# Batch 0's start in a fused attention and GEGLU kernel: small zero products, constants made in another order, masks put off, first gate block halved

## The chip, the cores and the metric

The kernel runs on one core of one Trainium2 chip. The metric is the device time of one execution, in microseconds, as the median of several executions. The core's engines run in parallel, each through its own queue in order: TensorE (PE, with its weight loads as PEld), VectorE (DVE), ScalarE (ACT), GpSimd (POOL), and SyncE (SP). POOL, ACT and SP also issue DMAs.

## What is computed

The reference is an attention block with a sliding window, followed by a gated feed-forward block, in float32:

```
scores = q @ k^T / sqrt(64) - slope[h] * |i - j|
attn   = softmax(scores where 0 <= i - j < 128)      # 8 batches, 8 heads, 576 positions, 64 wide
x      = (attn @ v), heads side by side               # 4608 tokens x 512
out    = (gelu(x @ w_gate) * (x @ w_val)) @ w_out     # 512 -> 1536 -> 512
```

## The kernel before, in words

All engines run in the order in which the program is written (`manual_schedule`, L52); nothing is reordered by a scheduler. Waits come from the data: an instruction waits for the producers of what it reads, and for the last readers of what it overwrites. PSUM has eight banks, taken in rotation by `bank()` (L70): taking a bank means waiting until the reads of its last content, eight takes before, are done.

The work has two interleaved streams. Attention goes batch by batch. Scores are held transposed (keys on partitions), 256 queries per 128 keys; `exp` on ACT (L211) writes them to `P` in bfloat16; a multiplication with `emask` on DVE (L214, `mask`) applies the slope and the window. The denominators are products of `P` with selecting constants (`ones4`, `ones8`, `sums4`, L342), then a reciprocal on DVE, then products with `sel` or `sel8` that spread the reciprocals over partitions (`spread4`, L383). `values` (L440) multiplies `P` with v and normalises into `xT`, the transposed tokens of the second stream. That stream goes by groups of 512 tokens: `gate_val(g, f, lo, hi)` (L467) makes one 128-row block f of the hidden layer, for the tokens lo to hi, from four products with w_gate and four with w_val, gelu on ACT (L481) and a product on DVE (L482); there are 12 blocks in a group. `out_part` (L495) makes the outputs. From batch 1 on, the mixing is written in `todo` and `steps`, which the change leaves alone.

Batch 0, where the change lies, is written out by hand at L526 to L645, to start the core as early as possible:

- Two lines load q and k in several pieces (`load_runs`), then v (`load_v`), then the weights (`load_w`), all from POOL. Each uses one of eight completion slots in turn, so a DMA is issued only when the DMA eight places before has landed.
- PE first runs products of zeros while nothing has landed: `keep_busy(8)` at L607 makes the next `bank()` issue 8 products of 128x512.
- DVE makes constants: memsets, `ident`, `dist`, `slopes` (L543 to L561). ACT makes `emask[:, h, 0:256]` (L553).
- `first` (L596) transposes q and k for positions 0 to 383 on PE and copies them from PSUM on DVE (`untangle`, L164). Batch 0's first scores get their bias as a product (`biases0`, L256) and need no mask.
- `made_later` (L570) on DVE: two memsets of padding, the copies of `emask` to columns 256 to 511, `sel0`, `sel`.
- `rest` (L601) does the same as `first` for positions 384 to 575; `made_last_part` (L580): `sel8`, `ones8`.
- `scores0_rest` (L275): the scores of the second part, with their exponentials and, at once, their masks. `sums4(0, 0)`, `products_first` and `spread_first` (L453, L458) give xT for tokens 0 to 383. Then come gate blocks f = 0, 1, 2 for these 384 tokens, with the second part's `sums4(0, 1)`, `spread4(0, 1)` and `values(0, 1)` between them, then blocks 0, 1, 2 for tokens 384 to 511 (L644), and from f = 3 whole blocks of 512.

Of the kernel before, what the change touches and what calls it, by code (L numbers as in the profile page):

```python
# [8 lines left out]
BF16 = mybir.dt.bfloat16  # L9
AF = mybir.ActivationFunctionType  # L10
ALU = mybir.AluOpType
# [21 lines left out]
def kernel(  # L33
# [10 lines left out]
    nc = tc.nc  # L44
# [25 lines left out]
    def bank():  # L70
        ps = psum.tile([128, 512], FP32, name="ps")
        for _ in range(heat.pop()):
            nc.tensor.matmul(out=ps.rearrange("p (n x) -> p n x", n=4), lhsT=zeros,
                             rhs=zeros.unsqueeze(1).to_broadcast((128, 4, 128)),
                             start=True, stop=True)
        heat.append(0)
        return ps

    def keep_busy(n):
        heat[0] = n  # L80
# [5 lines left out]
    ident = consts.tile([128, 128], BF16, name="ident")  # L86
# [8 lines left out]
    ones8 = consts.tile([128, 4 * 40], BF16, name="ones8")  # L95


    emask = consts.tile([128, H, 512], BF16, name="emask")
    sel0 = consts.tile([128, 8], FP32, name="sel0")
    sel = consts.tile([128, 8, 64], FP32, name="sel")  # L100
    sel8 = consts.tile([128, 4, 64], FP32, name="sel8")
# [4 lines left out]
    qT, kT = ([consts.tile([128, 4, 640], BF16, name=f"{nm}T{i}") for i in range(2)]  # L106
              for nm in "qk")
    vb = [consts.tile([128, 5, DM], BF16, name=f"vb{i}") for i in range(2)]
# [22 lines left out]
    def runs(what, b, n):  # L131
        first, parts, r = RUNS[b][n]
        t, lo, p = (qs, ks)[what][b], 1536 * n, 0
        if (b, n) == (0, 1):
            t, lo, p = vb[1], 0, 64 * what
        return t.rearrange("p j x -> p (j x)")[p:p + parts, lo:lo + 512 * r].rearrange(
            "p (h x) -> p h x", h=H)
# [15 lines left out]
    def transpose_runs(b, n, what, c, ps):  # L153
        first, parts, r = RUNS[b][n]
        src = runs(what, b, n)
        p = 64 * what if (b, n) == (0, 1) else 0
        for x in range(r):
            for i in (0, 1):
                nc.tensor.transpose(
                    out=ps[64 * i:64 * i + 64, parts * x:parts * x + parts],  # L160
                    in_=src[:, 2 * c + i, 64 * x:64 * x + 64],
                    identity=ident[p:p + parts, p:p + parts])

    def untangle(copy, b, n, what, c0, c1, ps):  # L164
        first, parts, r = RUNS[b][n]
        m = c1 - c0
        copy(out=(qT, kT)[what][b][:, c0:c1, first:first + parts * r].rearrange(  # L167
                 "p c (x r) -> p c x r", r=r),
             in_=ps[:, 0:m * parts * r].rearrange("p (c r x) -> p c x r", c=m, r=r))
# [43 lines left out]
    def mask(dst, m):  # L213
        nc.vector.tensor_tensor(out=dst, in0=dst, in1=m, op=ALU.mult)  # L214
# [41 lines left out]
    def biases0(cs):  # L256
        pss = []
        for c in cs:
            ps = [bank(), bank()]
            pss.append(ps)  # L260
            for i in (0, 1):
                bias(2 * c + i, ps[i], 2)
        return pss
# [8 lines left out]
                exp(prob(0)[:, c, i, 0:512], ps[i])  # L272


    def scores0_rest(cs):  # L275
        pss = []
        for c in cs:
            ps = [bank(), bank()]
            pss.append(ps)
            for j, q0, n, col in ((2, 384, 128, 0), (3, 384, 192, 128), (4, 512, 64, 320)):  # L280
                for i in (0, 1):
                    score(0, c, i, j, q0, n, ps[i][:, col:col + n])
        P = prob(0)
        for c, ps in zip(cs, pss):
            for i in (0, 1):
                exp(P[:, c, i, 640:1024], ps[i][:, 0:384])
            mask(P[:, c, :, 640:1024], emask[:, 2 * c:2 * c + 2, 128:512])


    def biases0_2():  # L290
# [6 lines left out]
    def scores0_2(pss):  # L297
        for c in range(4):
            for i in (0, 1):
                added(c, i, 2, 256, 128, pss[i][:, 128 * c:128 * c + 128])  # L300
        for i in (0, 1):
            exp(prob(0)[:, :, i, 512:640], pss[i].rearrange("p (c n) -> p c n", c=4))
# [164 lines left out]
    def gate_val(g, f, lo=0, hi=512, later=None):  # L467
        if g not in hid:
            hid[g] = h_pool.tile([128, NF, 512], BF16, name="hT")
        t0 = 512 * g % RING  # L470
        n = hi - lo
        pg, pv = bank()[:, 0:n], bank()[:, 0:n]
        for w, ps in ((wg, pg), (wv, pv)):
            for c in range(4):
                nc.tensor.matmul(  # L475
                    out=ps, lhsT=w[:, c, 128 * f:128 * (f + 1)],
                    rhs=xT[:, c, t0 + lo:t0 + hi], start=(c == 0), stop=(c == 3))

        def act():
            gl = g_pool.tile([128, 512], BF16, name="gelu")  # L480
            nc.scalar.activation(out=gl[:, 0:n], in_=pg, func=AF.Gelu)  # L481
            nc.vector.tensor_tensor(out=hid[g][:, f, lo:hi], in0=pv, in1=gl[:, 0:n],  # L482
                                    op=ALU.mult)

        if later is None:
            act()
        else:
            later.append(act)
# [37 lines left out]
    zeros = consts.tile([128, 128], BF16, name="zeros")  # L526
# [16 lines left out]
        nc.vector.memset(slope1[:, h:h + 1], -8.0 * 2.0 ** (-8.0 * (h + 1) / H))  # L543
    nc.vector.memset(ones4, 0.0)
    nc.vector.memset(ones4.rearrange("p (h x) -> p h x", x=36)[:, :, 0:4], 1.0)
    nc.vector.tensor_single_scalar(out=ident, in_=tmpl[:, 0:128], scalar=0.0, op=ALU.is_equal)
    for lo, bound, op in ((0, 0.0, ALU.is_lt), (128, 127.5, ALU.is_gt)):
        nc.vector.tensor_scalar(out=far[:, lo:lo + 128], in0=tmpl[:, lo:lo + 128],
# [7 lines left out]
    def made_slopes(lo, hi):  # L556
        nc.vector.tensor_tensor(
            out=slopes[:, lo:hi, :], in0=ident.unsqueeze(1).to_broadcast((128, hi - lo, 128)),
            in1=slope1[:, lo:hi].unsqueeze(2).to_broadcast((128, hi - lo, 128)), op=ALU.mult)
# [7 lines left out]
        load_runs(1, n, 0, 8)  # L567
    load_w(1280, DFF)

    def made_later():  # L570
        nc.vector.memset(kT[0][:, :, 576:640], 0.0)
        nc.vector.memset(vb[0][64:128, 4, :], 0.0)
        for to, lo, n in ((256, 0, 192), (448, 0, 64)):
            nc.vector.tensor_copy(out=emask[:, :, to:to + n], in_=emask[:, :, lo:lo + n])
        nc.vector.tensor_reduce(
            out=sel0, in_=ident.rearrange("p (g h r) -> p h g r", g=4, r=4)[:, :, :, 0],
            op=ALU.add, axis=mybir.AxisListType.X)
        nc.vector.tensor_copy(out=sel, in_=sel0.unsqueeze(2).to_broadcast((128, 8, 64)))

    def made_last_part():  # L580
        nc.vector.tensor_copy(
            out=sel8, in_=sel0[:, 0:8:2].unsqueeze(2).to_broadcast((128, 4, 64)))
        nc.vector.memset(ones8, 0.0)
        nc.vector.memset(ones8.rearrange("p (h x) -> p h x", x=40)[:, :, 0:8], 1.0)

    def made_last():
        nc.vector.memset(ones, 0.0)
        for i, lo, hi in ((0, 0, 4), (1, 4, 8), (0, 8, 16), (1, 16, 32)):
            nc.vector.memset(ones[:, i, lo:hi], 1.0)
        nc.vector.memset(kT[1][:, :, 576:640], 0.0)  # L590
        nc.vector.memset(vb[1][64:128, 4, :], 0.0)


    act, dve = nc.scalar.copy, nc.vector.tensor_copy

    def first(w, c, copy, ps):  # L596
        ps = ps.bitcast(BF16)
        transpose_runs(0, 0, w, c, ps)
        untangle(copy, 0, 0, w, c, c + 1, ps)
# [4 lines left out]
            transpose_runs(0, 1, w, c, ps[:, 192 * n:192 * n + 192])  # L604
        untangle(copy, 0, 1, w, cs[0], cs[-1] + 1, ps)

    keep_busy(8)  # L607
    held = [bank() for _ in range(4)]
    for c in (0, 1):
        first(0, c, dve, held[c])  # L610
    ps0 = biases0((0,))
    for c in (0, 1):
        first(1, c, dve, held[2 + c])
    made_slopes(4, 8)
    ps0 += biases0((1,))
    scores0((0, 1), ps0)
    held = [bank() for _ in range(4)]
    for w in (0, 1):
        for c in (0, 1):
            first(w, 2 + c, dve, held[2 * w + c])  # L620
    ps0 = biases0((2, 3))
    made_later()
    scores0((2, 3), ps0)
    ps0 = biases0_2()
    scores0_2(ps0)
    for cs in ((0, 1), (2, 3)):
        for w in (0, 1):
            rest(w, cs, dve)
    made_last_part()
    row(0)  # L630
    scores0_rest((0,))
    sums4(0, 0, False)
    scores0_rest((1,))
    products_first(range(4), (act, dve, act, dve))
    spread_first()
    scores0_rest((2, 3))
    masks = []
    gate_val(0, 0, 0, 384)
    sums4(0, 1, False)
    gate_val(0, 1, 0, 384)  # L640
    spread4(0, 1, (act, dve, act, dve))
    values(0, 1)
    gate_val(0, 2, 0, 384)
    for f in range(3):  # L644
        gate_val(0, f, 384, 512)  # L645
    for n in range(2):
        nc.gpsimd.dma_start(
            out=wo[:, 6 * n:6 * n + 6, :],
            in_=moe_w_out[768 * n:768 * n + 768, :].rearrange("(c p) f -> p c f", p=128))
# [120 lines left out]
```

## Time and profile before

| | |
|---|---|
| median of 4 runs | 355.14 us (353.86 to 355.89) |
| the profiled execution | 354.45 us, of which 352.7 us are the span of the trace |
| instructions in the span | 6763, of which 2724 products and 2724 weight loads on PE |
| first product of zeros, first transpose, first gate product | 1.00, 4.93, 21.27 us |
| HBM traffic over the span | 151 GB/s |
| granted TensorE clock | full in each slice that the page shows |

Times in the views count from the start of the span. A line of the timeline gives start, length, engine, source line, operation, result and operands, shape, how many instructions are merged (x12), and in brackets how long the engine was idle before it and what ended that. "issue" there means that the profile shows nothing that the engine waited for. The DMA view gives, for each queue, packets, MB, and the time that the packets took as a share of 16 engines over the window asked for.

### The profile page before, as it was taken

To read this page: it belongs to the slowest core of one execution; us is meant where nothing else is said; L and a number is where in the kernel's file an instruction comes from. 1 tells how busy PE (TensorE), PEld (TensorE's weight loads), DVE (VectorE), ACT (ScalarE), POOL (GpSimd) and SP (SyncE) were. 2 spreads that over 40 slices of the span, in tenths; PEclk is the share of its full clock that TensorE was granted. 3 is DMA by queue.
4 is the path that set the end of the run, shared out by engine and by line. 5 is a ranking of instruction groups with operands and counts; after the bars stand their busy time and mean duration, and the time that the engine had idled before them with its cause. 6 is when DMAs were issued, how large, how long until landed. Compare 5 with 4: busy or idle time off the path is not lost.

```text
span 352.7 us, 6763 instructions
## 1 busy us (share of the span) xinstructions
PE 343.0 (97%) x2724; PEld 168.4 (48%) x2724; DVE 193.1 (55%) x343; ACT 177.8 (50%) x325; POOL 107.2 (30%) x141
## 2 busy tenths in 40 slices
PE   8789999999999999999999999999999999999996
PEld 3455555544454445445444544445444444444443
DVE  6875468443878846854657566745674304403320
ACT  5653486536878365633963287237832233313322
POOL 8874662590940175001930094004000000000000
PEclk9999999999999999999999999999999999999999
DMA  9999999999998099964999599969206020011002
GB/s 104 163 196 191 205 160 185 179 143 179 140 155 178 5 144 188 197 124 89 135 207 158 109 117 205 153 134 97 91 4 134 32 89 0 4 62 57 2 26 92
DMA packets 148799, 42.61 MB, mean 121 GB/s; under 512 B 134776, under 2 KB 141688, under 8 KB 148768
## 3 DMA queue, kind: packets, MB, share of 16 engines
q0 software_dynamic: 109536, 18.88, 69.4%
q1 hardware_dynamic: 36432, 17.31, 20.9%
q10 hardware_dynamic: 2800, 5.99, 8.0%
q8 instruction: 21, 0.34, 0.4%
q14 instruction: 10, 0.08, 0.1%
HBM read 43.65 MB, written 9.53 MB: 151 GB/s over the span
## 4 chain that ended last, share of the span: by engine, by line
PE 88%; DMA 4%; DVE 3%; ACT 2%; POOL 2%; issue 0%; POOLq 0%; ACTq 0%; DVEq 0%
PE ps L475 53%; PE ps L501 24%; PE ps L433 4%; PE ps L207 3%; DMA vb<-in_k_dram 2%; DMA wg<-in_moe_w_gate_dram 1%; ACT P L211 1%; DVE P L214 1%; PE ps L402 1%; PE ps L380 1%; PE ps L517 1%; DVE xT L447 1%; PE ps L366 1%; DVE S L314 1%; POOL qs L142 0%
## 5 line engine op out<-in xcount | busy, mean ns | idle before, releaser
L482 DVE TENSOR_TENSOR hT<-ps,gelu 128x512 bf16<-128x512 f32 (+2 forms) x111 | 73.5, 673 | 101.0 <-PE ps L475 90.5
L481 ACT ACTIVATE gelu<-ps 128x512 bf16<-128x512 f32 (+2 forms) x111 | 64.4, 585 | 115.9 <-PE ps L475 113.6
L475 PE MATMUL ps<-xT,wg 128*128 128x512 bf16 (+2 forms) x444 | 111.6, 374 | 1.8 <-DMA wg<-in_moe_w_gate_dram 1.6
L475 PE MATMUL ps<-xT,wv 128*128 128x512 bf16 (+2 forms) x444 | 111.4, 373 | 0.0
L501 PE MATMUL ps<-wo,hT 128*128 128x512 bf16 x420 | 95.7, 380 | 0.0
L211 ACT ACTIVATE P<-ps 128x512 bf16<-128x512 f32 (+1 forms) x130 | 65.9, 614 | 8.1 <-PE ps L207 6.2
L475 PEld LDWEIGHTS <-wv 128*128 128x128 bf16 x444 | 43.0, 98 | 50.4
L475 PEld LDWEIGHTS <-wg 128*128 128x128 bf16 x444 | 41.7, 98 | 50.5 <-issue 2.9
L501 PEld LDWEIGHTS <-hT 128*128 128x128 bf16 x420 | 39.0, 98 | 46.6 <-issue 1.7
L214 DVE TENSOR_TENSOR P<-P,emask 128x1024 bf16<-128x1024 bf16 (+1 forms) x60 | 39.7, 679 | 23.8 <-ACT P L211 23.6
L506 ACT COPY osb<-ps 128x512 f32<-128x512 f32 x32 | 19.2, 599 | 35.5 <-PE ps L501 33.1
L116 POOL DMA_DIRECT2D vb<-in_v_dram x40 | 33.9, 902 | 5.1 <-PE ps L475 1.8
L447 DVE TENSOR_TENSOR xT<-ps,rb 128x320 bf16<-128x320 f32 (+2 forms) x64 | 22.9, 422 | 14.1 <-DMA rb<-rd 9.4
L720 POOL COPY mark<-hT 1x2 bf16<-1x2 bf16 x4 | 0.7, 174 | 93.1 <-DVE hT L482 93.1
L116 POOL DMA_DIRECT2D qs<-in_q_dram x30 | 25.2, 860 | 7.3 <-DMA wo<-in_moe_w_out_dram 5.9
L116 POOL DMA_DIRECT2D ks<-in_k_dram x30 | 25.4, 896 | 5.0 <-DMA qs<-in_q_dram 4.9
L433 PE MATMUL ps<-P,vb 128*64 128x256 bf16 (+3 forms) x384 | 18.3, 240 | 1.4 <-issue 1.3
L207 PE MATMUL ps<-qT,kT 64*128 64x256 bf16 (+3 forms) x352 | 18.7, 236 | 0.5 <-DVE kT L167 0.3
L407 DVE RECIPROCAL r<-ps 128x256 f32<-128x256 f32 (+1 forms) x10 | 18.8, 1922 | 0.0
L433 PEld LDWEIGHTS <-vb 128*64 128x64 bf16 x384 | 14.9, 110 | 7.0 <-issue 6.2
L207 PEld LDWEIGHTS <-kT 64*128 64x128 bf16 x352 | 12.0, 94 | 10.4 <-issue 8.5
L314 DVE TENSOR_TENSOR S<-P 128x1024 bf16<-128x1024 bf16 (+3 forms) x27 | 15.1, 590 | 0.5
(76 smaller groups left out, 132.6 us busy)
## 6 DMA issues: line engine op xcount, KB each, us to landing
out_dram<-osb SPq DMA_DIRECT2D x35, 256.0 KB, 2.6
rb<-rd ACTq DMA_DIRECT2D x10, 576.0 KB, 7.5
vb<-in_v_dram POOLq DMA_DIRECT2D x32, 128.0 KB, 6.5
qs<-in_q_dram POOLq DMA_DIRECT2D x24, 128.0 KB, 5.1
ks<-in_k_dram POOLq DMA_DIRECT2D x24, 128.0 KB, 5.7
wo<-in_moe_w_out_dram POOLq DMA_DIRECT2D x2, 768.0 KB, 14.9
wg<-in_moe_w_gate_dram POOLq DMA_DIRECT2D x5, 256.0 KB, 8.4
wv<-in_moe_w_val_dram POOLq DMA_DIRECT2D x5, 256.0 KB, 8.9
```

What stands on the lines that cost most here:

```text
L116: nc.gpsimd.dma_start(out=t[0:n, j, :].rearrange("p (h d) -> p h d", h=H), in_=src[b][:, 128 * j:128 * j + n, :].rearrange("h p d -> p h d"))
L207: nc.tensor.matmul(out=out, lhsT=columns(kT, b, i, c, 128 * j, 128), rhs=rhs, start=True, stop=True)
L211: nc.scalar.activation(out=dst, in_=src, func=AF.Exp, scale=0.125)
L214: nc.vector.tensor_tensor(out=dst, in0=dst, in1=m, op=ALU.mult)
L407: nc.vector.reciprocal(row(b)[:, lo:hi], ps[:, 0:hi - lo])
L433: nc.tensor.matmul(out=ps[64 * i:64 * i + 64, a - lo:e - lo], lhsT=vb[b % 2][:, j, 64 * h:64 * h + 64], rhs=P[:, c, i, col:col + e - a], s ...
L447: nc.vector.tensor_tensor(out=xT[:, c, at:at + e - a], in0=ps[:, a - lo:e - lo], in1=recip[b][:, c, a:e], op=ALU.mult)
L475: nc.tensor.matmul(out=ps, lhsT=w[:, c, 128 * f:128 * (f + 1)], rhs=xT[:, c, t0 + lo:t0 + hi], start=(c == 0), stop=(c == 3))
L481: nc.scalar.activation(out=gl[:, 0:n], in_=pg, func=AF.Gelu)
L482: nc.vector.tensor_tensor(out=hid[g][:, f, lo:hi], in0=pv, in1=gl[:, 0:n], op=ALU.mult)
L501: nc.tensor.matmul(out=acc[g], lhsT=hid[g][:, f, 128 * t:128 * (t + 1)], rhs=wo[:, f, :], start=(f == 0), stop=(f == NF - 1))
L506: (nc.vector.tensor_copy if t == 0 and g < 2 or t == 1 and g == 0 else nc.scalar.copy)(out=osb, in_=acc[g])
```

## The change

Five things change, all in batch 0's start.

- The products of zeros are 64 of 64 columns instead of 8 of 512.
- The memsets of `ones8`, of kT's padding and of v's padding (both batches') move to the first memsets on DVE; `sel0` is made right after `slopes`. The copies of `emask` to columns 256 to 511 are done in two halves of four heads, one after the first q copies, one before `rest`. `sel` and `sel8` are copied by ACT instead of DVE.
- The second four transposes (chunks 2 and 3 of q and k) are all issued before their copies, and the copies go q, k, q, k.
- The masks of the second part are collected and applied after `spread_first`: those of chunks 0 and 1, and then, after their scores, those of chunks 2 and 3.
- Gate block f = 0 for tokens 0 to 383 is made as 0 to 191 and 192 to 383; `sums4(0, 1)` comes after block f = 1, and block f = 2 comes ahead of `spread4(0, 1)` and `values(0, 1)`.

PE has 128 instructions more in all: 56 products of zeros and 8 gate products, each with its weight load.

```diff
         for _ in range(heat.pop()):
-            nc.tensor.matmul(out=ps.rearrange("p (n x) -> p n x", n=4), lhsT=zeros,
-                             rhs=zeros.unsqueeze(1).to_broadcast((128, 4, 128)),
-                             start=True, stop=True)
+            nc.tensor.matmul(out=ps[:, 0:64], lhsT=zeros, rhs=zeros[:, 0:64], start=True, stop=True)
...
-    def scores0_rest(cs):
+    def scores0_rest(cs, later):
...
-            mask(P[:, c, :, 640:1024], emask[:, 2 * c:2 * c + 2, 128:512])
+            later.append((P[:, c, :, 640:1024], emask[:, 2 * c:2 * c + 2, 128:512]))
...
+    nc.vector.memset(ones8, 0.0)
+    nc.vector.memset(ones8.rearrange("p (h x) -> p h x", x=40)[:, :, 0:8], 1.0)
+    for t in (kT[0], kT[1]):
+        nc.vector.memset(t[:, :, 576:640], 0.0)
+    for t in vb:
+        nc.vector.memset(t[64:128, 4, :], 0.0)
...
-    def made_later():
...
-    def made_last_part():
...
+    nc.vector.tensor_reduce(
+        out=sel0, in_=ident.rearrange("p (g h r) -> p h g r", g=4, r=4)[:, :, :, 0],
+        op=ALU.add, axis=mybir.AxisListType.X)
+
+    def masks_of_last_blocks(lo, hi):
+        for to, at, n in ((256, 0, 192), (448, 0, 64)):
+            nc.vector.tensor_copy(out=emask[:, lo:hi, to:to + n], in_=emask[:, lo:hi, at:at + n])
...
-    keep_busy(8)
+    keep_busy(64)
     held = [bank() for _ in range(4)]
     for c in (0, 1):
         first(0, c, dve, held[c])
     ps0 = biases0((0,))
+    masks_of_last_blocks(0, 4)
     for c in (0, 1):
         first(1, c, dve, held[2 + c])
+    nc.scalar.copy(out=sel, in_=sel0.unsqueeze(2).to_broadcast((128, 8, 64)))
     made_slopes(4, 8)
     ps0 += biases0((1,))
     scores0((0, 1), ps0)
     held = [bank() for _ in range(4)]
-    for w in (0, 1):
-        for c in (0, 1):
-            first(w, 2 + c, dve, held[2 * w + c])
+    for w, c in ((0, 0), (0, 1), (1, 0), (1, 1)):
+        transpose_runs(0, 0, w, 2 + c, held[2 * w + c].bitcast(BF16))
+    for w, c in ((0, 0), (1, 0), (0, 1), (1, 1)):
+        untangle(dve, 0, 0, w, 2 + c, 3 + c, held[2 * w + c].bitcast(BF16))
     ps0 = biases0((2, 3))
-    made_later()
     scores0((2, 3), ps0)
     ps0 = biases0_2()
     scores0_2(ps0)
+    masks_of_last_blocks(4, 8)
     for cs in ((0, 1), (2, 3)):
         for w in (0, 1):
             rest(w, cs, dve)
-    made_last_part()
     row(0)
-    scores0_rest((0,))
+    masks = []
+    scores0_rest((0,), masks)
     sums4(0, 0, False)
-    scores0_rest((1,))
+    scores0_rest((1,), masks)
     products_first(range(4), (act, dve, act, dve))
     spread_first()
-    scores0_rest((2, 3))
-    masks = []
-    gate_val(0, 0, 0, 384)
+    for args in masks:
+        mask(*args)
+    masks.clear()
+    scores0_rest((2, 3), masks)
+    for args in masks:
+        mask(*args)
+    nc.scalar.copy(out=sel8, in_=sel0[:, 0:8:2].unsqueeze(2).to_broadcast((128, 4, 64)))
+    masks.clear()
+    for lo in (0, 192):
+        gate_val(0, 0, lo, lo + 192)
+    gate_val(0, 1, 0, 384)
     sums4(0, 1, False)
-    gate_val(0, 1, 0, 384)
+    gate_val(0, 2, 0, 384)
     spread4(0, 1, (act, dve, act, dve))
     values(0, 1)
-    gate_val(0, 2, 0, 384)
     for f in range(3):
         gate_val(0, f, 384, 512)
```

More of the change, by code (lines that the diff above doesn't have):

```diff
@@ L568 @@
     load_w(1280, DFF)
-    def made_later():
[L571 to L578, printed above, removed]
-    def made_last_part():
[L581 to L584, printed above, removed]
+    nc.vector.tensor_reduce(
[4 more added lines that the diff above has]
+            nc.vector.tensor_copy(out=emask[:, lo:hi, to:to + n], in_=emask[:, lo:hi, at:at + n])
     def made_last():
@@ L589, in made_last @@
             nc.vector.memset(ones[:, i, lo:hi], 1.0)
-        nc.vector.memset(kT[1][:, :, 576:640], 0.0)
-        nc.vector.memset(vb[1][64:128, 4, :], 0.0)
     act, dve = nc.scalar.copy, nc.vector.tensor_copy
```

## The prediction

> **What bounds the kernel now.** I read the page first, then the timeline by engine over the first 30 us (the only part that the diff touches), then the DMA view in narrow windows, then the order of the instructions with their waits.
>
> ```profile
> PE 343.0 (97%) x2724; PEld 168.4 (48%) x2724; DVE 193.1 (55%) x343; ACT 177.8 (50%) x325; POOL 107.2 (30%) x141
> ...
> PE 88%; DMA 4%; DVE 3%; ACT 2%; POOL 2%; issue 0%; POOLq 0%; ACTq 0%; DVEq 0%
> ```
> TensorE is the bound: 88% of the chain. Asked for PE's waits from 30 us to the end, the trace names one of 0.2 us. So what matters is when PE enters its unbroken stretch (the 128-column gate products at 27.31), and that date should carry through to the end. PE's timeline before it:
>
> ```profile
> 12.80 0.56 PE L159 MATMUL ps<-ident,vb 64*64 64x64 bf16 x36 [0.37 <-DMA vb<-in_k_dram]
> ...
> 14.06 0.96 PE L366 MATMUL ps<-P,ones 128*32 128x96 bf16 x64
> 14.95 0.34 PE L207 MATMUL ps<-qT,kT 64*128 64x128 bf16 x6
> 15.23 0.41 PE L433 MATMUL ps<-P,vb 128*64 128x256 bf16 x3
> 16.97 1.15 PE L433 MATMUL ps<-P,vb 128*64 128x256 bf16 x21 [1.33 <-issue]
> 18.04 1.15 PE L380 MATMUL ps<-r,sel 32*128 32x96 f32 x32
> 19.12 0.51 PE L207 MATMUL ps<-qT,kT 64*128 64x128 bf16 x12
> 21.27 0.81 PE L475 MATMUL ps<-xT,wg 128*128 128x384 bf16 x4 [1.64 <-DMA wg<-in_moe_w_gate_dram]
> ```
> Two holes. The second is put down to the gate weights, but these landed 6.5 us after their issue at 8.72, at 15.3, and their first weight load runs at 19.56: PE waits for the normalised xT.
>
> ```profile
> 19.27 1.95 DVE L461 TENSOR_TENSOR xT<-rb,ps 128x384 bf16<-128x384 f32 x4 [0.56 <-PE ps L380]
> 21.14 1.02 DVE L214 TENSOR_TENSOR P<-P,emask 128x768 bf16<-128x768 bf16 x2
> ```
> The first hole stops the fourth value product, which waits for no semaphore; v's third block landed at 14.8 (its issue near 7.9, plus 6.9 to landing). What fits is the fetch of instructions:
>
> ```profile
> q0 software_dynamic: 70, 0.02, 174.2%
> q8 instruction: 1, 0.02, 60.9%
> ```
> This is the DMA view of 14.6 to 14.7: one packet of 16 KB on the instruction queue (60.9% of 16 engines x 0.1 us: 0.97 us long). There are 21 in the span for 2 x 2724 PE instructions: one per 256. Before the hole lie 220 products and 220 loads, then 4 loads and 3 products; with the opening branch that is 448 = 512 - 64: the end of a block, if 64 instructions precede the kernel. PE passed the block's start (192) at 11.2 to 12.05, the packet began at 14.6 (2.6 to 3.4 later), ended at 15.6, and PE went on at 16.97, 1.4 after it. The next crossing (16.97) has its packet at 20.8 (3.9 later); one near 59.6 has it at 63.9 (4.3).
>
> [...] By the row a late block costs 1.33 us. I follow the row: the stop falls on the block's end.
>
> **The change, part by part.**
>
> Zero products: 8 of 512 columns become 64 of 64, the same 4096 columns. Before: one per 0.43 us, ending at about 4.4. Nearest row for short ones: L366, 64 load-product pairs in 0.96 us, so no floor per product near 53 ns. I take 64 x 0.053 = 3.4 us, done before q lands (4.93). Below: no gain, q's landing waits. Above: 0.08 each (load not overlapped), end at 6.1. That delay and the next two meet PE's hard date, k's rest rows at 12.80, and vanish there. What remains is 112 more PE instructions, so block ends sit 112 instructions earlier in the work.
>
> DVE constants: memsets of ones8, kT and vb (0.12 + 0.09 + 2 x 0.17 + 2 x 0.27 = 1.0 us) go into DVE's idle 1.45 to 3.38; the 0.19 reduction precedes the q copies; half of the emask copies (1.03/2 = 0.52) precedes the first kT copies. Queued behind: first kT copies at 7.3 instead of 6.55, scores and exponentials 0.7 late. From 10.60 DVE loses 0.17 + 0.27 + 0.52 + 0.19 + 0.43 = 1.6 us before the rest copies, yet these still need the transposes at 12.05 and 12.80: gain 0 to 0.2. Cover: k's landing.
>
> sel and sel8 on ACT: 0.43 and 0.28 on DVE, by the nearest ACT row (0.52 for a 384-column copy) at most 0.7 and 0.35 there. sel stands at 7.2, in ACT's wait for the first scores (at 8.1 now), and delays nothing; without that wait it would delay each exponential by 0.7. sel8 stands between the last exponentials (19.6) and the gelu table's load (1.28): gelus from 21.3 instead of 20.9, while DVE works at masks until 21.7.
>
> [...] The emask half would stand beside v's issues at 6.12 to 8.72. The nearest row, a 0.74 us issue at 11.34 beside the emask copies of 11.14 to 12.17, is no longer than others (0.73 to 0.83). [...] I take 0.
>
> The fetch: block end 448 now falls in the first sums (L366), reached at about 14.2. Its fetch starts at PE's passing 192, now the last product of the first scores, at 7.9. Plus 2.6 to 4.3 plus 2.4 gives 12.9 to 14.6: no stall, 0.4 at worst. Products start at 15.25 and don't stop: 1.7 us earlier. Spread 16.4 to 17.55 (reciprocal done at 16.0, ACT's copies at 17.3), xT 17.6 to 19.55 instead of 19.27 to 21.22.
>
> First gate block in halves: the first needs only two xT pieces: 18.64, 8 x 0.082 = 0.66, to 19.3; the second could start at 19.6. But the next block end, 704, is now the first half's last product. Crossing 448 at 14.15 plus 3.5 (between 2.6 and 4.3; nearest 3.4 and 3.9) plus 2.4 gives 20.0 (19.1 to 20.9). So a stall of 0.8 stands at 19.2, and the second half starts at 20.05.
>
> Masks put off: four of 0.52 on DVE after xT, to 21.7 instead of two to 22.16. Behind them wait the hT products and PE's second sums. PE then: second half to 20.7, f=1 (1.40, as from 23.17 to 24.57) to 22.1, sums (0.5) to 22.6, f=2 24.0, spread (0.63) 24.65, value products (0.80) 25.45. DVE: three hT (0.33, 0.33, 0.56, the last after f=1's products end at 22.3) to 22.95, reciprocal (0.75) 23.7, hT of f=2 (products end 24.2) 24.75, copies (0.62) 25.4, xT (1.14) 26.55. The gate of f=2, which covered this last xT work (26.00 to 27.31), now stands ahead of the spread, and nothing covers it. The banks that f=2, the spread and the products take are freed by gelu and hT results named above, each before its taker's date, the tightest being hT of f=2 for the fourth products (24.75 against 25.25). Before, the fourth 128-column product began at 27.31 + 3 x 0.055 = 27.48, now at 26.6: **0.9 us earlier**, at least 1.25 with no stall at 704.
>
> Afterwards: landings of weights stay where POOL's own queue puts them, since only DMA slots and early waits hold it. The tightest is wo's second half, landing at 46.4 (issue 30.14 and 16.3) for a product at 48.5 now and 47.6 after. Of later blocks only 1472 to 1728 is short (6.3 us of work near 58): 0 to 0.5.
>
> **Sum.** Own time 354.45 (span 352.67 and 1.8 around it) less 0.9 = 353.55; against the median 355.14, which is 0.7 above that execution, 354.2.
>
> **The rivals.**
> A, forecast: stall moved and smaller, 0.3 to 1.2 gained, 354.2. Chance 0.55.
> B: the block at 704 comes in time: 1.25 gained and up to 0.2 from DVE, 353.8. For it: the third packet followed its boundary by 2.3. Against: 3.9 at the nearest crossing. 0.17.
> C, slower: the hole isn't fetch and stays, so xT still ends at 21.22, and the four masks bind DVE: masks to 23.35, three hT 24.5, reciprocal 25.25, hT 26.05, copies 26.7, xT 27.85, PE's fourth product at 27.9: 0.4 late, 355.5. It decides once xT ends after about 20.8. [...] 0.14.
> D: latency of 6.9 or more at the first crossing: 1 us of stall in the sums and 2 at 704: 0.6 late, 355.7. Against: the longest seen is 4.3 + 2.4. 0.08.
> The change then doesn't do what it says if early clock or zeros differ: nothing moves, 355.1: 0.06.
>
> **Numbers.** 0.5% (1.78 us, about what a measurement of this kernel can tell from no change) lies beyond every case's centre. But four runs cover 2.0 us, so a median is known to some 0.5 and more between sessions: B and A's better end pass the bound at 0.25; C, D or an unseen wait pass it upwards at 0.12. Within: 0.63. The range holds A to D with that scatter: 352.6 to 356.0.
>
> **What would show it.** Right: no issue hole in L433; one of 0.4 to 1.2 us in the first 192-column gate; packets near 11 and 17.6; xT from 17.6; fourth 128-column product at 26.2 to 27. Wrong: L433 still at 16.97 (C), a hole in the sums (D), first transposes after 5.5 (zeros dearer), or new PE waits past 30 us that take the gain back.

## The result and the profile after

The median after is 353.03 us (41 executions between 352.48 and 354.81, and one of 588.01, whose granted TensorE clock was 0.558 in the mean, where the others had 0.995 or more); before, in 63 executions, it is 354.62 (353.05 to 358.64). The ratio is 0.9951, interval 0.994 to 0.9962: 1.7 us less by the ratio, 1.6 by the two medians. The forecast was 0.9 us less. The profiled executions have spans of 352.7 and 350.9 us.

The page of the kernel after, its first and its fourth part (busy time, and the chain that ended last by engine):

```profile
PE 343.1 (98%) x2788; PEld 171.2 (49%) x2788; DVE 193.4 (55%) x344; ACT 178.5 (51%) x328; POOL 107.6 (31%) x141
...
PE 90%; DVE 3%; ACT 2%; DMA 2%; POOL 1%; issue 1%; POOLq 0%; ACTq 0%; DVEq 0%
```

PE is busy for the same 343 us, with 64 more products, in a span that is 1.8 us shorter. What went is idle time. PE's timeline of the kernel after shows where:

```profile
15.36 1.29 PE L431 MATMUL ps<-P,vb 128*64 128x256 bf16 x24
16.57 1.15 PE L378 MATMUL ps<-r,sel 32*128 32x96 f32 x32
...
18.87 0.49 PE L473 MATMUL ps<-xT,wg 128*128 128x192 bf16 x4 [0.71 <-DVE xT L459]
...
19.80 0.50 PE L473 MATMUL ps<-xT,wg 128*128 128x192 bf16 x4
...
25.76 1.01 PE L473 MATMUL ps<-xT,wg 128*128 128x128 bf16 x4 [0.43 <-DVE xT L445]
```

All 24 value products run as one row from 15.36; before, three ran, then 1.33 us went by. The spread follows at 16.57 instead of 18.04, the first gate block at 18.87 instead of 21.27. There is no "issue" hole ahead of the second half (19.80) either; its first weight load waited 0.34 us for xT. The fourth 128-column product starts at 26.55 (it is the last of the row at 25.76, whose first three came before a wait of 0.43); before, it was 27.48. So PE's unbroken stretch begins 0.93 us earlier.

DVE's timeline of the kernel after, for the same stretch:

```profile
17.80 1.95 DVE L459 TENSOR_TENSOR xT<-rb,ps 128x384 bf16<-128x384 f32 x4 [0.56 <-PE ps L378]
19.66 1.96 DVE L212 TENSOR_TENSOR P<-P,emask 128x768 bf16<-128x768 bf16 x4
...
24.36 0.56 DVE L480 TENSOR_TENSOR hT<-ps,gelu 128x384 bf16<-128x384 f32 x1 [0.91 <-PE ps L473]
...
25.36 1.14 DVE L445 TENSOR_TENSOR xT<-ps,rb 128x192 bf16<-128x192 f32 x4
```

xT is made from 17.80 instead of 19.27, all four masks behind it are done at 21.62, and the last xT ends at 26.5. PE now waits for this last xT, as the prediction said, and no other work covers it.

The DMA view of 10.3 to 10.4, and then of 16.1 to 16.2, shows the packets of instructions:

```profile
q8 instruction: 1, 0.02, 59.2%
```

```profile
q8 instruction: 1, 0.02, 59.1%
```

Before, the same two packets began at 14.60 and 20.83. Counted as in the prediction, PE's second, third and fourth block start at the 96th, the 224th and the 352nd product. The first packet (10.33) follows PE's entry into the block before it (8.0) by 2.3 us, and the second (16.14) follows the crossing at 14.35 by 1.8. With 0.94 us for the packet and the 1.4 that passed before between the end of a packet and PE's next instruction, the next block should be there at 18.5 by this estimate, ahead of its need at 19.4.

0.93 us is half of the 1.8 that the spans differ by. If the products of the two traces are laid side by side, another 0.84 appears between 164 and 168 us, where DVE waits for the broadcast of a later batch's reciprocals. The waits of DVE in the kernel before and then after (both 150 to 175 us; sum, count, longest):

```profile
DVE xT L447 <- DMA rb<-rd: 3.6, 1, 3.6
```

```profile
DVE xT L445 <- DMA rb<-rd: 1.4, 1, 1.4
```

The change does not touch that place. Two further profiles of the kernel before have no such loss: from the fourth 128-column product to the end of the span they take 324.4 and 324.35 us, the first took 325.19, and after takes 324.35. So the 0.84 belongs to the one execution that was profiled first, not to the kernel, and the gain has to be looked for at the entry.

### The profile page after: what moved, and what is told of

The parts are those of the page before. It is cut to its first block, busy times and chain, and to the rows that moved or that the text cites. A ratio compares the mean times of both kernels' runs of the same rounds, so it can differ in the third digit from the quotient of the medians.

```text
span 350.9 us, 6898 instructions
## 1 busy us (share of the span) xinstructions
PE 343.1 (98%) x2788; PEld 171.2 (49%) x2788; DVE 193.4 (55%) x344; ACT 178.5 (51%) x328; POOL 107.6 (31%) x141
## 3 DMA queue, kind: packets, MB, share of 16 engines
q0 software_dynamic: 109536, 18.88, 69.8%
## 4 chain that ended last, share of the span: by engine, by line
PE 90%; DVE 3%; ACT 2%; DMA 2%; POOL 1%; issue 1%; POOLq 0%; ACTq 0%; DVEq 0%
PE ps L473 54%; PE ps L499 24%; PE ps L431 4%; PE ps L205 3%; DMA vb<-in_k_dram 2%; ACT P L209 1%; PE ps L364 1%; PE ps L378 1%; DVE P L212 1%; PE ps L400 1%; PE ps L515 1%; DVE S L312 1%; DVE xT L459 1%; PE ps L157 1%; POOL qs L140 0%
## 5 line engine op out<-in xcount | busy, mean ns | idle before, releaser
L480 DVE TENSOR_TENSOR hT<-ps,gelu 128x512 bf16<-128x512 f32 (+3 forms) x112 | 74.1, 668 | 103.2 <-PE ps L473 97.3
L479 ACT ACTIVATE gelu<-ps 128x512 bf16<-128x512 f32 (+3 forms) x112 | 64.5, 582 | 115.6 <-PE ps L473 110.7
L473 PE MATMUL ps<-xT,wg 128*128 128x512 bf16 (+3 forms) x448 | 112.2, 372 | 1.5 <-DVE xT L459 0.7
L473 PE MATMUL ps<-xT,wv 128*128 128x512 bf16 (+3 forms) x448 | 111.6, 372 | 0.0
L504 ACT COPY osb<-ps 128x512 f32<-128x512 f32 x32 | 19.2, 600 | 35.4 <-PE ps L499 33.1
L431 PE MATMUL ps<-P,vb 128*64 128x256 bf16 (+3 forms) x384 | 17.6, 240 | 0.0
```

What stands on the lines that cost most here:

```text
L431: nc.tensor.matmul(out=ps[64 * i:64 * i + 64, a - lo:e - lo], lhsT=vb[b % 2][:, j, 64 * h:64 * h + 64], rhs=P[:, c, i, col:col + e - a], s ...
L473: nc.tensor.matmul(out=ps, lhsT=w[:, c, 128 * f:128 * (f + 1)], rhs=xT[:, c, t0 + lo:t0 + hi], start=(c == 0), stop=(c == 3))
L504: (nc.vector.tensor_copy if t == 0 and g < 2 or t == 1 and g == 0 else nc.scalar.copy)(out=osb, in_=acc[g])
```

## Experiments

### Is the first hole a fetch? Four sizes of the zero products

The zero products are the one place where the number of PE's instructions can be changed with the same number of columns: 8 of 512 (before), 16 of 256, 32 of 128, 64 of 64 (after). Each pair more is two instructions, and moves every end of a block by two.

**The changed kernel with the old zero products.** All the rest of the change stays.

```diff
-            nc.tensor.matmul(out=ps[:, 0:64], lhsT=zeros, rhs=zeros[:, 0:64], start=True, stop=True)
+            nc.tensor.matmul(out=ps.rearrange("p (n x) -> p n x", n=4), lhsT=zeros,
+                             rhs=zeros.unsqueeze(1).to_broadcast((128, 4, 128)), start=True, stop=True)
...
-    keep_busy(64)
+    keep_busy(8)
```

> The changed kernel with one thing undone: 8 zero products of 512 columns again. Fetch theory (a block of 256 PE instructions ends at the 448th and the next comes 4.3 to 5.7 us after its forerunner was entered): the block end lies on the fourth value product again, so PE stops there from about 15.4 to 17.0, xT ends near 21.3, and with four masks behind it DVE brings the fourth 128-column product to about 28.2, against 27.48 before: 0.7 us slower than before, ratio 1.002. Rival (the stop is set by the order of work, by masks and constants, not by instruction counts): like the changed kernel, no stop, ratio 0.995.

Measured: 355.17 us against 354.76 for the kernel before on the same chip, ratio 1.0026 (0.9999 to 1.0052). PE's timeline:

```profile
15.74 0.41 PE L433 MATMUL ps<-P,vb 128*64 128x256 bf16 x3
18.01 1.15 PE L433 MATMUL ps<-P,vb 128*64 128x256 bf16 x21 [1.86 <-issue]
```

The hole is back, ahead of the same fourth product. It lasts to 18.01 where 17.0 was expected, and the last xT finds no cover, so the fourth 128-column product starts at 29.07 (28.2 expected). With the hole, the rest of the change gains nothing; the 0.4 us that the medians lose cannot be told from none by the interval.

**The kernel before with 64 small zero products**, and nothing else:

```diff
-            nc.tensor.matmul(out=ps.rearrange("p (n x) -> p n x", n=4), lhsT=zeros,
-                             rhs=zeros.unsqueeze(1).to_broadcast((128, 4, 128)), start=True, stop=True)
+            nc.tensor.matmul(out=ps[:, 0:64], lhsT=zeros, rhs=zeros[:, 0:64], start=True, stop=True)
...
-    keep_busy(8)
+    keep_busy(64)
```

> The kernel before with only the zero products changed (64 of 64 columns). Fetch theory: the block end moves into the first sums, entered at 7.2 and there by 12, so no stop in the value products (15.25 to 16.5), xT ends at 19.6, and the old order of gate, sums and spread, in which PE is never short of work, starts the fourth 128-column product at about 25.9: 1.6 us earlier than before and 0.6 earlier than the changed kernel, ratio 0.9955 or less. Rival (zero products only keep the clock, same columns, same end): nothing, ratio 1.000, stop from 15.6 to 17.0.

Measured: 353.37 us, ratio 0.9974 (0.9954 to 0.9995). PE's timeline:

```profile
15.30 1.29 PE L431 MATMUL ps<-P,vb 128*64 128x256 bf16 x24
...
19.94 0.81 PE L473 MATMUL ps<-xT,wg 128*128 128x384 bf16 x4 [1.76 <-DVE xT L459]
...
25.98 0.39 PE L473 MATMUL ps<-xT,wg 128*128 128x128 bf16 x4
```

This one edit removes the hole, and its profile enters the long stretch at 26.15, earlier than the whole change does; 25.9 was expected. But this execution (352.34 us) is the fastest of the twelve. The median gains 1.4 us, where at least 1.6 was expected, and less than the whole change.

**16 of 256 and 32 of 128**, in the kernel before:

```diff
-            nc.tensor.matmul(out=ps.rearrange("p (n x) -> p n x", n=4), lhsT=zeros,
-                             rhs=zeros.unsqueeze(1).to_broadcast((128, 4, 128)),
+            nc.tensor.matmul(out=ps[:, 0:256].rearrange("p (n x) -> p n x", n=2), lhsT=zeros,
+                             rhs=zeros.unsqueeze(1).to_broadcast((128, 2, 128)),
...
-    keep_busy(8)
+    keep_busy(16)
```

and the same with `out=ps[:, 0:128]`, `rhs=zeros`, `keep_busy(32)`.

> The kernel before with 16 zero products of 256 columns: same columns, 16 PE instructions more. Fetch theory: the block end moves by 16 instructions, to the score products of the second part (the group ahead of the value products), entered at nearly the same time (11.2 to 11.7), so the stop starts there at about 15.0 and ends at about 16.8; no stop in the value products; time like before within 0.3 us, ratio 1.000. Rival (v's arrival or a bank): the stop stays at the fourth value product.

> The kernel before with 32 zero products of 128 columns: same columns, 48 PE instructions more. Fetch theory: the block end moves into the later part of the first sums, reached at about 14.8; its forerunner is entered at about 10.2, so it comes at 14.5 to 15.9: a stop of 0 to 1.1 us inside the sums, none in the value products; 0.5 to 1.6 us earlier than before, ratio 0.9955 to 0.9985, between e3 and e2. Rival: nothing, ratio 1.000.

Measured: 356.93 us, ratio 1.0072 (1.0045 to 1.01), and 354.79 us, ratio 0.9991 (0.9967 to 1.0014). PE's timelines, first 16 of 256, then 32 of 128:

```profile
14.99 0.23 PE L207 MATMUL ps<-qT,kT 64*128 64x128 bf16 x1
17.51 0.47 PE L207 MATMUL ps<-qT,kT 64*128 64x128 bf16 x5 [2.29 <-issue]
17.91 2.35 PE L433 MATMUL ps<-P,vb 128*64 128x256 bf16 x24
```

```profile
14.57 0.74 PE L364 MATMUL ps<-P,ones 128*32 128x96 bf16 x49
17.04 0.49 PE L364 MATMUL ps<-P,ones 128*32 128x96 bf16 x15 [1.73 <-issue]
...
17.73 2.19 PE L431 MATMUL ps<-P,vb 128*64 128x256 bf16 x24
```

Both holes stand where counting puts them: 16 instructions further on in the count is 16 earlier in the work, after one product of the six scores; 48 earlier is after 49 of the 64 sums. A wait for data would not move by the count of zero products. Three sizes give a hole at three places, each at the counted instruction, and the fourth size gives none. The packets agree: in all six profiles with the hole (these two, the changed kernel with the old zero products, and the three of the kernel before) PE goes on 1.4 to 1.7 us after the end of the one packet that comes then, 5.1 to 6.2 us after it entered the block before. That the hole is the end of PE's block is shown.

Both times missed, though, for two reasons. The holes were longer than expected: they ended at 17.51 (16.8 expected), and lasted 1.73 us (1.1 at most expected). And the value products after the hole took 2.35 and 2.19 us, 1.29 in the kernel after: PE ran at half its clock (0.50 granted, next section).

### Half clock

The stretches of the 16-of-256 kernel and then of the 32-of-128 kernel; the first of the last three columns is the granted clock:

```profile
15.50:16.00 0.50, 0.00 (x0) 0.00 (x0) 0.50 (x2) 0.00 (x0) 0.50 (x2) 0.83 1.93 157
...
22.50:23.00 0.50, 0.38 (x10) 0.30 (x7) 0.50 (x2) 0.31 (x1) 0.40 (x1) 0.85 1.46 193
```

```profile
17.50:18.00 0.50, 0.50 (x13) 0.37 (x13) 0.44 (x1) 0.17 (x1) 0.50 (x2) 0.94 1.49 197
...
21.00:21.50 0.50, 0.50 (x20) 0.50 (x12) 0.00 (x0) 0.00 (x0) 0.50 (x2) 0.65 1.48 194
```

All slices between the two of each kernel are at 0.50, and those outside at 1.00. A slice of 0.83 dates the step: 0.17/0.5 of it, 0.17 us, is at half clock. So the first kernel runs at half clock from 15.83 to 22.65, 6.82 us, and the second from 17.94 to 21.35, 3.41 us, half as long. The clock does not answer to the hole directly: in one case it falls 0.6 us after PE stopped, in the other 0.9 us after PE had resumed, and the kernel with the 1.86 us hole above kept full clock. What sets the length of these stretches is not shown. In the 3.41 us that led up to the half clock PE was busy for 2.19 us (from 12.41) in the 16-of-256 kernel, and for 1.68 us (from 14.53) in the 32-of-128 kernel. These runs give no threshold of work either: in the kernel with the 1.86 us hole PE was busy for 1.54 of the 3.40 us from 15.00, and for as much of the 3.40 us from 15.80, and the clock stayed full (1.00).

Each execution's mean clock tells the same without a profile: it was 0.989 in the profiled execution with 6.82 us at half clock, and 0.995 in the one with 3.41 us, as one or two stretches of 3.41 us in 352 us make it (0.995 and 0.990). It does not tell when the stretch came. Counted over the executions whose clock is on record (one is left out, the 588.01):

| kernel | executions | with a half-clock stretch | median at full clock, us |
|---|---|---|---|
| before | 79 | 30 | 354.40 |
| before, 16 of 256 | 7 | 7 | none |
| before, 32 of 128 | 12 | 10 | 353.62 |
| before, 64 of 64 | 12 | 6 | 353.10 |
| after, 8 of 512 | 12 | 4 | 354.93 |
| after, both groups | 54 | 4 | 352.99 |
| after, masks at once | 8 | 0 | 352.45 |
| after, old gate order | 12 | 0 | 352.52 |
| before, 64 of 64 and halves, both groups | 12 | 0 | 352.17 |

The 353.62 rests on two executions. At full clock 64 small products gain 1.30 us by themselves, less than the 1.9 between their profile's entry (26.15) and the mean entry of the kernel before (28.0, below): the profiled execution lies 0.76 under this row's median. In the kernel before a half-clock stretch goes with about 1.0 us (355.41, the median of the 27 executions with one such stretch, less 354.40).

The rows speak against the fetch hole as the only cause of these stretches. The changed kernel with the old zero products has the hole and waits 0.71 us for xT: 4 of 12. The kernel before with 64 small products has no hole but waits 1.76 us for xT: 6 of 12. The kernel before has both: 30 of 79. The kernel after has no hole and waits 0.71 us: 4 of 54. So each of the two idle times seems to bring such stretches, but this is argued from counts. Masks at once, the old gate order and half of the last row ran on another chip, where the kernel before itself had a stretch in 4 of 19 executions, against 26 of 60 on the first; their zeros count for less.

### How far the hole itself scatters

Two more profiles of the kernel before and one of the kernel after, unchanged.

> The kernel before once more, for a second profile. Fetch theory: the stop is again at the fourth value product, but its length follows the DMA traffic of the moment (1.3 to 2.3 us), and where it is long the clock falls to half for some us. The late broadcast of reciprocals near 164 us (0.84 us that the first profile of before lost, and no other profile so far) should be absent.

> The kernel before, third profile. If the stop's length is what scatters its time, value products go on anywhere between 16.9 and 18, and the time follows that date.

> The changed kernel once more on this chip, to compare with the version above: fourth 128-column product at 26.4 to 26.7, no stop, ratio 0.995.

Measured: 354.13 and 354.68 us (one execution each), and 353.22 us for after, ratio 0.9964 (0.994 to 0.9988). PE's timelines of the two kernels before:

```profile
15.43 0.41 PE L433 MATMUL ps<-P,vb 128*64 128x256 bf16 x3
17.49 1.15 PE L433 MATMUL ps<-P,vb 128*64 128x256 bf16 x21 [1.65 <-issue]
```

```profile
15.82 0.41 PE L433 MATMUL ps<-P,vb 128*64 128x256 bf16 x3
18.03 1.15 PE L433 MATMUL ps<-P,vb 128*64 128x256 bf16 x21 [1.81 <-issue]
```

The hole was 1.33 us in the first profile and is 1.65 and 1.81 here, and the clock stayed full, where half clock had been expected after a long hole; the fourth 128-column product starts at 28.0 and 28.55, against 27.48. After, it starts at 26.55 and 26.38. The means, 28.01 and 26.47, are 1.5 us apart, which is the gain at full clock (354.40 less 352.99: 1.41).

### The other parts of the change

**Masks at once**, as before; all the rest of the change stays.

```diff
-            later.append((P[:, c, :, 640:1024], emask[:, 2 * c:2 * c + 2, 128:512]))
+            mask(P[:, c, :, 640:1024], emask[:, 2 * c:2 * c + 2, 128:512])
```

> The changed kernel with the masks of the second part applied at once, as before. If deferring pays (the masks delay the way to xT): chunk 1's mask stands ahead of the product copies on DVE, xT ends 0.35 us later, at about 20.1, two masks follow to 21.1 instead of four to 21.6, and the fourth 128-column product starts at about 26.9, 0.35 later than in the changed kernel, ratio 0.996. If instead the four masks behind xT are what binds: it starts at about 26.1, ratio 0.994.

Measured: 352.44 us, ratio 0.9945 (0.9924 to 0.9966). PE's timeline:

```profile
18.88 0.49 PE L473 MATMUL ps<-xT,wg 128*128 128x192 bf16 x4 [0.83 <-DVE xT L459]
...
25.49 1.01 PE L473 MATMUL ps<-xT,wg 128*128 128x128 bf16 x4 [0.20 <-DVE xT L445]
```

The first gate half starts at 18.88 (18.87 with the masks put off): two masks more ahead of xT delay nothing, because with the masks put off DVE waits there for the spread (0.56 us). Behind xT there are two fewer, and the fourth product starts at 26.28 instead of 26.55 and 26.38. Putting the masks off brings nothing here.

**The old order of the gate blocks**: sums, f = 1, spread, values, f = 2, again with all the rest of the change.

```diff
-    gate_val(0, 1, 0, 384)
     sums4(0, 1, False)
-    gate_val(0, 2, 0, 384)
+    gate_val(0, 1, 0, 384)
     spread4(0, 1, (act, dve, act, dve))
     values(0, 1)
+    gate_val(0, 2, 0, 384)
```

> The changed kernel with the old order of gate blocks, sums and spread after the two halves. Theory (masks end at 21.6 whatever PE does, so sums wait): PE idles about 1.2 us before the sums, but the gate of f=2 covers the last xT work again: the fourth 128-column product starts at 26.4 to 26.7, as in the changed kernel, ratio 0.995. If the new gate order gains by itself: 0.5 us later, ratio 0.9965.

Measured: 352.52 us, ratio 0.9948 (0.9931 to 0.9964). PE's timeline:

```profile
21.25 0.91 PE L364 MATMUL ps<-P,ones 128*32 128x96 bf16 x39 [0.42 <-DVE P L212]
...
26.24 0.39 PE L473 MATMUL ps<-xT,wg 128*128 128x128 bf16 x4
```

A wait of 0.42 for the masks ahead of the sums takes the place of the 0.43 for the last xT, and the fourth product starts at 26.41. The new order moves the wait, and saves nothing.

**The kernel before with 64 small zero products and the first gate block in halves**, nothing else of the change; it ran twice. To the diff of the 64 small products above comes

```diff
-    gate_val(0, 0, 0, 384)
+    for lo in (0, 192):
+        gate_val(0, 0, lo, lo + 192)
```

> The kernel before with only two parts of the change: 64 small zero products and the first gate block in halves; constants, masks and order as before. Theory (the zero products remove the fetch stop, the halves use the hole before xT's end, the rest is neutral or costs): the first half starts at about 18.9, the fourth 128-column product at about 25.5, 1.0 us earlier than in the changed kernel, ratio 0.9925 to 0.994, unless the block end that falls near it (704) stops PE. Rival (constants or masks carry part of the gain): 26.6 or later, ratio 0.995 or more.

> The kernel before with small zero products and the halves only, once more: if it is the best version, ratio 0.992 to 0.9945, below the changed kernel's 0.9951, and the fourth 128-column product between 25.4 and 26.0; if its first measurement was luck, 0.995 or more.

Measured: 352.04 us, ratio 0.9931 (0.9908 to 0.9954), and 352.24 us, ratio 0.9928 (0.9902 to 0.9953). PE's timeline in the second:

```profile
19.22 0.49 PE L473 MATMUL ps<-xT,wg 128*128 128x192 bf16 x4 [0.82 <-DVE xT L459]
...
25.67 0.39 PE L473 MATMUL ps<-xT,wg 128*128 128x128 bf16 x4
```

These two edits alone are the fastest version of all: the fourth product starts at 25.96 and 25.84, some 0.6 us before that of the whole change. The halves cut PE's wait for xT from 1.76 to 0.82 us. No execution of twelve had a half-clock stretch (six of them on the first chip), where six of twelve had one without the halves. Against the whole change (0.9951, 0.994 to 0.9962, and 0.9964, 0.994 to 0.9988) the intervals overlap a little; that this version is 0.7 to 1.0 us faster rests on the medians (352.24 against 353.22 on one chip, 352.17 against 352.99 at full clock) and on the entry.

**The change without its late masks and without its new gate order** (both edits above at once): what is left is the zero products, the constants, the grouped transposes, and the halves.

> The changed kernel with both its mask deferral and its new gate order undone: what is left is the small zero products, the constants and the halves. Against before_64_and_halves it adds only the constants. If the constants' moves are hidden (k's landing ahead of the rest transposes): the fourth 128-column product at 25.5 to 26.0 as there, ratio 0.993. If they pay: 25.3 or earlier, ratio below 0.992.

Measured: 352.77 us, ratio 0.9941 (0.9913 to 0.9968). PE's timeline:

```profile
7.52 0.53 PE L157 MATMUL ps<-ident,ks 128*64 128x128 bf16 x12 [1.35 <-DMA ks<-in_k_dram]
...
27.30 0.39 PE L473 MATMUL ps<-xT,wg 128*128 128x128 bf16 x4
```

In this execution k landed late and the clock was half from 7.94 to 11.35 (0.58 in the mean from 8 to 12), so its dates say nothing of the constants; the median lies 0.5 to 0.7 above the version without the new constants, with intervals that overlap. Whether the new order of the constants costs something stays open. The trace shows one thing more. PE crossed its block's end at 15.83, the packet began only at 19.02, 3.2 us later, and ended at 19.96; PE's weight loads then stopped at the next block's end, the last product of the first half:

```profile
20.80 0.26 PEld L473 LDWEIGHTS <-wv 128*128 128x128 bf16 x3
21.30 0.10 PEld L473 LDWEIGHTS <-wv 128*128 128x128 bf16 x1 [0.24 <-issue]
```

This is the stop that the prediction had placed there, with 0.24 us instead of 0.8.

## Why the prediction was right, and where not, point by point

**The hole is a fetch: right, and shown** by three sizes with the hole at three counted places, and a fourth without it. The packet came late here: before the change the packet of the block that PE needed at 15.64 began at 14.6, and at the first three block ends of every trace such a packet began only after PE had entered the block before it, by 1.8 to 3.9 us.

**The zero products: right.** 64 of 64 columns took 3.59 us, 8 of 512 took 3.60; 3.4 was forecast. They end before q lands, and the first transpose comes at 4.87.

**Constants: right in sum.** An `emask` half took 0.85 us, where half of the old copy gave 0.52. The delay meets the rest rows of k, whose transposes start at nearly the same time as before (12.93 for 12.80), as the cover that was named said. The `emask` half beside v's issues, put at 0, cost nothing there: v's three issues took 2.69 us beside it, and 2.69 before the change, without it. `sel` and `sel8` took 0.60 and 0.42 on ACT and delayed nothing that PE waited for.

**Products, spread and xT: right.** Forecast and measured: products 15.25 and 15.36, spread 16.4 and 16.57, xT 17.6 and 17.80, first half 18.64 and 18.87.

**"So a stall of 0.8 stands at 19.2": failed.** It did not come; PE passed the block's end at 19.4 without a stop, and the second half started at 19.80 instead of 20.05. The term that was mis-sized is the step from the crossing to the packet. It was put at 3.5 us, after the nearest crossings' 3.4 and 3.9; it was 1.8, and 2.8 in the second profile of after. That is rival B at this place. In the eight profiles with 64 small products the step is 1.8 to 3.2 us, and the 3.2 stopped PE for 0.24 (the last experiment): the place was right, the size was not. Why the packets come earlier here than after a hole (3.9 in the three profiles of before) stays open. The 4.3 at the upper end came from a crossing counted at 59.6, and so far out the count is not safe: the packet at 40.27 begins before the crossing that is counted at 41.03. The first three crossings of all profiles give 1.8 to 3.9.

**The entry: right as a number, for partly wrong reasons.** Forecast 26.6, measured 26.55. Without the stall at 704 the forecast chain gave 26.2 or before. What was late instead is hT of f = 2 on DVE: its products' signal came at 23.89 and it started at 24.36, 0.47 later, and 0.47 later in the second profile of after (23.71, 24.18) and with the old zero products too, but 0.07 with the masks at once or the old gate order. Two errors cancelled, which is luck. Why hT starts late there stays open.

**Masks put off and gate order: costed right, and worth nothing.** DVE finished the masks at 21.62 (21.7 forecast), and the last xT lost its cover as was said. The two parts undone one at a time show that each could have been left as it was.

**The size: 0.9 forecast, 1.6 to 1.7 measured.** The term that was mis-sized is the hole before the change. Its 1.33 us came from one profile, and that one had the shortest hole of three (1.33, 1.65, 1.81); the entry of before is 28.0 in the mean, not 27.48. That is 0.5 of the difference. The rest, some 0.2 on the median, is the half clock: a stretch of it in 30 of 79 executions before, in 4 of 54 after. That PE's idle times before the change bring these stretches on is argued from the counts; no profile of the kernel before caught one. The forecast had no half clock in it; the scatter between executions, which was put into the range, carried this.

Rivals C and D fall with the timeline: no hole at the fourth value product, none in the sums. The new waits past 30 us that would have made the prediction wrong did not appear; the one difference there, at 164 us, is in before's first profile alone.

## What to carry to other kernels

A hole that waits for nothing the profile shows deserves a count. Here 447 products and weight loads, 448 instructions with the opening branch, stood ahead of it, 64 short of 512, and the trace had one instruction packet per 256 or so (21 for 5448). Change the number of instructions ahead of such a hole by a few and see whether the hole moves by as many. A hole's length taken from one profile is one draw: profile the kernel two or three times before making a sum with it. And of a change with several parts, try each alone: here two of them hold more than the whole gain.

## What the runs showed of the hardware

- The instructions of PE came in packets of 16 KB, one per 256 or so (21 packets, 0.34 MB, for 5448 instructions before; 22 for 5576 after), and the hole moved by 16 and by 48 instructions as counting by blocks of 256 has it. A packet took 0.9 to 1.1 us at the first three block ends. Beside the loads of q, k, v and weights it began 1.8 to 3.9 us after PE's entry into the block before. In the seven stops seen (six holes, and the 0.24 us) PE went on 1.3 to 1.7 us after the packet's end, and 5.1 to 6.2 us after that entry. PE had run through the block that ended in the stop in under 4 us in the kernel before (from about 12 to 15.64); the block from 14.35 to 19.4 in the kernel after, 5.05 us, ended without one.
- PE's clock fell to half for 3.41 us (32 of 128, and the last experiment) or 6.82 us (16 of 256) at a stretch, with PE busy for 1.68 us (32 of 128) and 2.19 us (16 of 256) of the 3.41 before; it stayed full in the changed kernel with the old zero products after 1.54 us of work in 3.40. Nor does the hole's length decide: 1.73 us with half clock, 1.86 without.
- 64-column products with 128-column weights ran at 3.59/64 = 56 ns each at the start, while 512-column ones took 3.60/8 = 450 ns: the same columns, the same time. Later in the trace of before, 512-column products follow one another every 0.216 us (four from 28.65 to 29.52). So both kinds ran at about half the later pace at the start, although the view gives a granted clock of 1.00 there; no run here settles why.
